# A MoE kernel's startup: where the last decoded weight tiles put their scratch, and when four of them are decoded

## The chip, the cores and the metric

One core of a Trainium2 chip runs the whole program. The metric is the device time of one execution in microseconds; before the change it is 847.33 us, the median of three runs (847.04 to 848.21).

## What is computed

The reference is a delta-rule attention, followed by two mixture layers on its output:

```
for t in range(S):                       # 4 batches x 8 heads, S = 768, D = 48
    y[t]  = q[t] @ state
    state = state + beta[t] * outer(k_n[t], v[t] - k_n[t] @ state)
x   = y as 3072 tokens x 384
h   = ((x @ w1) * (x @ w2)) @ w3         # 384 -> 1024 -> 1024
x2  = h @ w_out                          # 1024 -> 384
e   = argmax(x2 @ w_gate + bias[modality])          # 8 experts, one per token
out = gate[e] * (relu(x2 @ e_w1[e]) @ e_w2[e])
```

The weights w1, w2, w3 and w_out are stored as 8-byte floats, the rest as 4-byte floats.

## The kernel before

**The stages.** `startup` (L528) loads and decodes the 8-byte weights, multiplies w3 with w_out ahead of time (so that only one product, called w34, is left), computes the first attention step and prepares the inverse matrices of the first two pairs of steps. Then `moe1` (L720) runs for twelve blocks of 256 tokens: block i computes x @ w1, x @ w2, their product and the product with w34 for the tokens of step i, while `slot` (L165) issues the attention of step i + 1 between these matmuls. At the end `moe2` runs the experts. Each block of `moe1` has eight parts, f = 0 to 7, called eighths here. An eighth takes 128 of the 1024 hidden columns: 18 matmuls into one PSUM tile `pAB` (two halves, w1 and w2), then ScalarE's copy `a`, VectorE's product `a`, ScalarE's cast `ch`, VectorE's remainder `cl`. Its six matmuls with w34 (`px`) follow two eighths later (LAG = 2).

**The order of instructions.** All five engines issue in the order in which the Python code is written (the class `Engine`, L77 to L91, chains every instruction to the one before on its engine, so all rows of the profile stand at L84). The order around the change is set by the list `todo` of 36 tiles (L543 to L549) and by `tick(n)` (L653), which decodes one of them:

- `issue` (L557) starts DMAs from the SP queue. A tile lands in a buffer `raw` that is borrowed: the six places that later hold the second halves of w1 and w2 (`w010` to `w112`), and `x0`, `x1`, `xr`. A place of the first kind can be borrowed only by tiles up to the one that will be stored there (`last`, L551), so the last tiles of the list have few places, and each waits for the decode that gives one back.
- `scalar(n + 1)` (L582) has ScalarE write two things for the next tile: its magnitude `mag` and its low words, the latter into one of four slots of the SBUF tile `TT[1]`, called `sc` (slot n % 4).
- `vector(n)` (L598) combines them with two VectorE instructions.
- `use(n)` (L606) consumes the decoded tile: a w3 tile is read by four matmuls (`pw`), each of the w1 and w2 tiles is split into a high part by ScalarE and a low part by VectorE one tick later (`flush`, L647).

The tiles of w3 and w1/w2 alternate from tile 16 on. Numbers in this text: tile 28 and tile 30 are the last two of w3, the tiles 29 and 31 to 35 are the six of the second half of w1 and w2 (needed from eighth 4 of block 0 on).

**Where mag lives.** Ten tiles use the PSUM pool `pc`. The others use the tag `AB`, two PSUM banks, the same two that `pAB` of all blocks uses. Only the last tile, 35, has it in a slot of `sc`, two slots away from its own:

```
if n < FC + 2:
    mag[n] = self.pc.tile([P, DCH], F32, tag="pc", name="mag")
elif n <= NSTART:
    mag[n] = pm.tile([P, DCH], F32, tag="AB", name="mag", bufs=2)
else:
    mag[n] = sc[:, (n + 2) % 4]
```

**What block 0 still decodes.** `REST = (1, 1)`: tile 34 in eighth 0 and tile 35 in eighth 1 of block 0. VectorE also takes steps of the inverse of the second pair of attention steps there (`self.work`; two tensor_tensor rows `tmp` and `Tt` each); `PLAN1` says how many in each eighth, 21 in all.

**What the SP queue holds behind the tiles.** After the DMA of tile 35 come two tiles of keys (`kb`), the queries `W` of step 1 and step 2 (two DMAs each, one for each half of the partitions), and the values of step 2 (`vt`). The queries of step 1 are read by the matmuls `pq`, which stand on TensorE between eighth 1 and eighth 2 of block 0.

Of the kernel before, what the change touches and what calls it, by code (L numbers as in the profile page):

```python
# [51 lines left out]
PLAN = (0, 0, 3, 4, 5, 2, 1, 3), (2, 0, 4, 3, 4, 2, 0, 1)  # L52

MID = (0,) * 5 + (0, 0, 1) + (2, 2, 2, 1, 1, 1, 1, 2)
PLAN1 = (3, 4, 4, 3, 3, 2, 1, 1)
WORK1 = {0: 2, 1: 2, 2: 3, 3: 3, 4: 3, 5: 3}
AHEAD, W0 = 8, 0
CHAIN, GRAMS = (1, 1, 1, 1, 1, 1), (-6, -5, -3, -2)
START0 = (3, 3, 3, 3, 3, 3, 3)

REST = (1, 1)
EARLY = {2: 1, 3: 1, 4: 2, 5: 4, 6: 4, 7: 4}
LEAD = 1
LAG = 2
# [39 lines left out]
class Kernel:  # L104
# [423 lines left out]
    def startup(self):  # L528
# [14 lines left out]
        todo = [("o", g) for g in range(FC)] + w3s[:AHEAD] + w12[:W0]  # L543
        w12, n = w12[W0:], 0
        for x in range(AHEAD, K3):
            k = x + 1 - AHEAD
            todo += [w3s[x]] + w12[n:k]
            n = k
        todo += w12[n:]  # L549
        NSTART = len(todo) - sum(REST)  # L550
        last = {f"w{m}1{kk}": todo.index(("w", (m, 1, kk))) for kk in range(KC) for m in range(2)}  # L551
# [30 lines left out]
        def scalar(n):  # L582

            if n < len(todo):
                L, Hw, _ = raw[n]
                if n < FC + 2:
                    mag[n] = self.pc.tile([P, DCH], F32, tag="pc", name="mag")
                elif n <= NSTART:
                    mag[n] = pm.tile([P, DCH], F32, tag="AB", name="mag", bufs=2)
                else:  # L590
                    mag[n] = sc[:, (n + 2) % 4]
                mag[n] = mag[n][:, :L.shape[-1]]

                nc.scalar.activation(mag[n], Hw.bitcast(F32), AF.Abs, scale=2.0 ** -112)

                nc.scalar.activation(out[n].bitcast(I32), L.bitcast(U32), AF.Copy, scale=2.0 ** -29 * (1 - 2.0 ** -16), bias=7.5 * 2.0 ** -16 - 0.5)

        def vector(n):  # L598
            L, Hw, tag = raw.pop(n)
            o, stt = out[n].bitcast(I32), nc.vector.scalar_tensor_tensor  # L600
            stt(out=o, in0=mag[n].bitcast(I32), scalar=3, in1=o, op0=ALU.logical_shift_left, op1=ALU.bitwise_or)
            stt(out=o, in0=Hw, scalar=-2147483648, in1=o, op0=ALU.bitwise_and, op1=ALU.bitwise_or)
            if tag != "x0" or n < FC:
                free.append(tag)
# [42 lines left out]
        def flush(n):  # L647
            now = [f for due, f in after if due <= n]
            after[:] = [x for x in after if x[0] > n]
            for f in now:  # L650
                f()

        def tick(n):  # L653
            self.n = n
            if n >= NSTART:
                flush(n)
            scalar(n + 1)
            vector(n)
            flush(n)
            issue()  # L660
            use(n)

        def split(g):

            next(g)
            after.append((self.n + 1, lambda: list(g)))
# [9 lines left out]
        for g in grams:  # L676
            next(g)
        do = {-1: [lambda: scalar(0)], 0: [lambda: list(grams[0])], 1: [lambda: list(grams[1]), lambda: list(grams[2])], 2: [lambda: list(grams[3])],
              FC - 4: [lambda: self.queries(0), lambda: self.values(0), self.routing_loads],
              FC - 2: [lambda: self.keys(1)],  # L680
              FC + 3: [lambda: split(self.masked(0))], FC + 5: [lambda: self.tokens(0), lambda: self.values(1)]}
# [12 lines left out]
        for x in range(0, NU, HP):  # L694
            do.setdefault(FC + len(START0) + GRAMS[x // HP], []).append(lambda x=x: split(self.gram(1, x)))
        c = FC + len(START0)
        do.setdefault(c + 1, []).append(lambda: setattr(self, "work", self.inverse(1)))
        for n, k in WORK1.items():
            do.setdefault(c + 1 + n, []).extend([lambda: next(self.work)] * k)
        rs = self.routing_setup()  # L700
        for x in range(3):
            do.setdefault(FC + 8 + x, []).append(lambda: next(rs, None))
# [2 lines left out]
        for n in range(-1, NSTART):  # L705
            if n >= 0:
                tick(n)
            for f in do.get(n, ()):
                f()

        def rest():
            for n in range(NSTART, len(todo)):
                tick(n)
                yield
            flush(len(todo))

        flush(NSTART)
        self.rest = rest()

    def moe1(self, i):  # L720
# [3 lines left out]
        for f in range(FC):  # L724
# [16 lines left out]
            nc.scalar.copy(ch, a)  # L741
            steps = (PLAN1 if i == 0 else PLAN[(i + LEAD) % US])[f]
            if steps:
# [15 lines left out]
            if f == 6 and i + 1 < NT // MT:  # L759
                self.parts_x(i + 1)  # L760
            for _ in range(REST[f] if i == 0 and f < len(REST) else 0):
                next(self.rest, None)
            if i == 0 and f == len(REST):
                list(self.rest)
# [590 lines left out]
```

## Time and profile before

| | |
|---|---|
| median of three runs | 847.33 us |
| the profiled execution's own time | 850.87 us |
| its span, first to last instruction | 849.2 us |
| TensorE (PE) busy | 796.1 us, 94% of the span |
| VectorE (DVE) busy | 610.1 us, 72% |
| ScalarE (ACT) busy | 407.1 us, 48% |
| mean granted TensorE clock | 0.968 of full speed |

Times in all rows are counted from the first instruction. PE means TensorE's matmuls and PEld its weight loads; a row of the timeline gives the start, the length, the engine, the operation with output and inputs, the shape, how many equal instructions it merges, and, in brackets, how long the engine was idle before it and what ended that. A plain fp32 matmul of the program appears as two PE rows. DMA rows on the SP queue show the issue, not the transfer.

### The profile page before, as it was taken

To read this page: it belongs to the slowest core of one execution; us is meant where nothing else is said; L and a number is where in the kernel's file an instruction comes from. 1 tells how busy PE (TensorE), PEld (TensorE's weight loads), DVE (VectorE), ACT (ScalarE), POOL (GpSimd) and SP (SyncE) were. 2 spreads that over 40 slices of the span, in tenths; PEclk is the share of its full clock that TensorE was granted. 3 is DMA by queue.
4 is the path that set the end of the run, shared out by engine and by line. 5 is a ranking of instruction groups with operands and counts; after the bars stand their busy time and mean duration, and the time that the engine had idled before them with its cause. 6 is when DMAs were issued, how large, how long until landed. Compare 5 with 4: busy or idle time off the path is not lost.

```text
span 849.2 us, 24808 instructions
## 1 busy us (share of the span) xinstructions
PE 796.1 (94%) x10223; PEld 739.2 (87%) x10223; DVE 610.1 (72%) x1517; ACT 407.1 (48%) x859; POOL 160.8 (19%) x167
## 2 busy tenths in 40 slices
PE   5796789999999999999999999999899999999994
PEld 5564459999999999999999999999899999999983
DVE  5998899669856975697589854467785678677651
ACT  6357573561446244615452353334454655555541
POOL 5001201100001000000100000003244654645420
PEclk8599899999999999999999999999999999999998
DMA  9843463203120412132112301037457778666610
GB/s 299 288 152 97 125 182 108 74 22 103 66 67 29 126 40 64 37 117 62 41 41 62 102 2 40 21 117 238 143 168 223 241 229 266 222 219 229 236 59 7
DMA packets 48777, 105.42 MB, mean 124 GB/s; under 512 B 9412, under 2 KB 28756, under 8 KB 48656
## 3 DMA queue, kind: packets, MB, share of 16 engines
q1 hardware_dynamic: 41424, 88.35, 33.3%
q0 software_dynamic: 4064, 11.06, 3.8%
q10 hardware_dynamic: 3168, 4.34, 1.4%
q8 instruction: 82, 1.34, 0.7%
q14 instruction: 39, 0.32, 0.1%
HBM read 89.15 MB, written 10.63 MB: 118 GB/s over the span
## 4 chain that ended last, share of the span: by engine, by line
PE 67%; DVE 12%; issue 9%; POOL 4%; ACT 4%; DMA 3%; SPq 0%; POOLq 0%; ACTq 0%; DVEq 0%
PE pAB L84 23%; PE px L84 13%; PE ph L84 7%; PE spy L84 4%; PE py L84 3%; PE pu L84 3%; PE pq L84 2%; PE pk L84 2%; PE pg L84 2%; PE pw L84 2%; DVE TT L84 2%; PE pS L84 2%; POOL w1l L84 2%; PE pe L84 1%; POOL out_dram L84 1%
## 5 line engine op out<-in xcount | busy, mean ns | idle before, releaser
L84 PE MATMUL pAB<-x,w 128*128 128x256 f32 x1728 | 231.3, 288 | 2.7 <-DVE a L84 2.6
L84 PEld LDWEIGHTS pAB<-x,w 128*128 128x128 f32 x1728 | 214.4, 191 | 7.0 <-DVE a L84 2.8
L84 DVE TENSOR_TENSOR a<-a,pAB 128x256 f32<-128x256 f32 x96 | 40.0, 417 | 84.7 <-ACT a L84 84.4
L84 ACT COPY a<-pAB 128x256 f32<-128x256 f32 x96 | 35.7, 372 | 134.4 <-PE pAB L84 113.7
L84 ACT CAST ch<-a 128x256 fp32r<-128x256 f32 x96 | 38.9, 406 | 104.6 <-DVE a L84 104.6
L84 PE MATMUL ph<-sxh,w1h 128*128 128x256 f32 x288 | 82.7, 287 | 0.5 <-DVE hl L84 0.5
L84 ACT ACTIVATE hh<-ph 128x256 fp32r<-128x256 f32 x96 | 37.0, 385 | 94.2 <-PE ph L84 93.9
L84 PE MATMUL ph<-sxh,w1l 128*128 128x256 f32 x288 | 81.6, 283 | 0.0
L84 PE MATMUL ph<-sxl,w1h 128*128 128x256 f32 x288 | 81.6, 283 | 0.0
L84 DVE SCALAR_TENSOR_TENSOR hl<-ph,hh 128x256 fp32r<-128x256 f32 x96 | 40.3, 419 | 42.9 <-ACT hh L84 41.6
L84 DVE TENSOR_TENSOR tmp<-Ab,Tt 128x31 f32<-128x31 f32 (+15 forms) x186 | 67.1, 361 | 3.0
L84 DVE TENSOR_TENSOR Tt<-tmp,Tt 128x31 f32<-128x31 f32 (+15 forms) x186 | 63.9, 343 | 6.4
L84 DVE TENSOR_TENSOR w2l<-r,w2h 128x768 fp32r<-128x768 f32 x56 | 58.7, 1060 | 12.5 <-ACT w2h L84 12.2
L84 PE MATMUL px<-w34h,ch 128*128 128x392 f32 x192 | 65.6, 342 | 0.0
L84 PE MATMUL px<-w34h,cl 128*128 128x392 f32 x192 | 65.3, 340 | 0.0
L84 PE MATMUL px<-w34l,ch 128*128 128x392 f32 x192 | 65.2, 339 | 0.0
L84 POOL TENSOR_TENSOR w1l<-r,w1h 128x512 fp32r<-128x512 f32 x39 | 51.1, 1328 | 49.8 <-ACT w1h L84 49.6
L84 PEld LDWEIGHTS ph<-sxh,w1h 128*128 128x128 f32 x288 | 54.9, 191 | 1.3 <-DVE hl L84 1.1
L84 PEld LDWEIGHTS ph<-sxh,w1l 128*128 128x128 f32 x288 | 55.2, 192 | 0.0
L84 PEld LDWEIGHTS ph<-sxl,w1h 128*128 128x128 f32 x288 | 54.9, 191 | 0.0
L84 DVE TENSOR_TENSOR cl<-a,ch 128x256 fp32r<-128x256 f32 x96 | 40.4, 421 | 20.1 <-ACT ch L84 19.3
L84 ACT CAST w1h<-r 128x512 fp32r<-128x512 f32 x84 | 49.4, 616 | 2.3 <-DMA r<-in_e_w_dram 1.9
(263 smaller groups left out, 1678.4 us busy)
## 6 DMA issues: line engine op xcount, KB each, us to landing
r<-in_e_w_dram SPq DMA_DIRECT2D x42, 512.0 KB, 4.8
r<-in_e_w_dram SPq DMA_DIRECT2D x56, 384.0 KB, 3.9
raw<-in_w_dram SPq DMA_DIRECT2D x28, 512.0 KB, 3.9
kT<-in_kt_dram SPq DMA_DIRECT2D x12, 512.0 KB, 4.6
W<-in_q_dram SPq DMA_DIRECT2D x24, 256.0 KB, 4.2
vt<-in_v_dram SPq DMA_DIRECT2D x12, 384.0 KB, 4.2
kb<-in_kb_dram SPq DMA_DIRECT2D x12, 384.0 KB, 3.2
x2d<-xr ACTq DMA_DIRECT2D x22, 192.5 KB, 2.9
```

Source lines behind the costliest of these rows:

```text
L84: x = f(*a, **kw)
```

## The change

Tile 31 onward has its magnitude in `sc` instead of an `AB` bank. Four tiles instead of two are decoded in block 0: one in eighth 0, one in eighth 1, two in eighth 2. The list is reordered so that the last two tiles of w3 come as tiles 28 and 29, and the six tiles of the second half of w1 and w2 follow as tiles 30 to 35. From tile 30 on a tick first flushes what is due (the split of the tile before), then decodes. The steps of the inverse in block 0 are dealt out anew, 21 as before.

```diff
-PLAN1 = (3, 4, 4, 3, 3, 2, 1, 1)
+PLAN1 = (2, 2, 1, 4, 4, 4, 4, 0)
...
-REST = (1, 1)
+REST = (1, 1, 2)
+W0S = 1
...
         for x in range(AHEAD, K3):
-            k = x + 1 - AHEAD
+            k = min(x + 1 - AHEAD, 6)
             todo += [w3s[x]] + w12[n:k]
             n = k
...
-                elif n <= NSTART:
+                elif n < NSTART - 1:
                     mag[n] = pm.tile([P, DCH], F32, tag="AB", name="mag", bufs=2)
                 else:
                     mag[n] = sc[:, (n + 2) % 4]
...
         def tick(n):
             self.n = n
-            if n >= NSTART:
+            if n >= NSTART - 2:
                 flush(n)
             scalar(n + 1)
             vector(n)
...
-        do.setdefault(c + 1, []).append(lambda: setattr(self, "work", self.inverse(1)))
+        do.setdefault(c + W0S, []).append(lambda: setattr(self, "work", self.inverse(1)))
         for n, k in WORK1.items():
-            do.setdefault(c + 1 + n, []).extend([lambda: next(self.work)] * k)
+            do.setdefault(c + W0S + n, []).extend([lambda: next(self.work)] * k)
...
-        flush(NSTART)
         self.rest = rest()
```

NSTART is the number of tiles less the sum of REST: 34 before, 32 now. W0S = 1 leaves the start of the second inverse where it was. One line more at the top of the file makes L84 into L85.

The order of the rows on TensorE, on the SP queue and on GpSimd is the same as before, name by name; what differs there is which tile a `raw` or `pw` row belongs to. ScalarE and VectorE are reordered, and the prediction speaks of three places.

ScalarE, end of startup, from the magnitude of tile 32 to the first copy `a` of block 0 (`mag` is a PSUM bank, `TT_95` is `sc`, a CAST to `w_...` is the high part of a w1 or w2 tile), before:

```order
L84 ACTIVATE mag<-raw 128x512
L84 ACTIVATE TT_95<-raw 128x512
L84 ACTIVATE mag<-raw 128x512
L84 ACTIVATE TT_95<-raw 128x512
L84 CAST w_1184<-TT_95 128x512
L84 ACTIVATE mag<-raw 128x512
L84 ACTIVATE TT_95<-raw 128x512
L84 CAST w_1192<-TT_95 128x512
L84 CAST w34h<-pw 128x392
L84 CAST w_1200<-TT_95 128x512
L84 COPY a<-pAB 128x256
```

The same place in the change, from the magnitude of tile 30:

```order
L85 ACTIVATE mag<-raw 128x512
L85 ACTIVATE TT_95<-raw 128x512
L85 CAST w34h<-pw 128x392
L85 ACTIVATE TT_95<-raw 128x512 x2
L85 CAST w_1173<-TT_95 128x512
L85 ACTIVATE TT_95<-raw 128x512 x2
L85 COPY a<-pAB 128x256
```

The two rows "x2" are magnitude and low words of tile 31 and of tile 32, both now in `sc`. Tile 33 and tile 34 are no longer ahead of block 0.

VectorE, from the remainder `R` of attention step 1 through eighth 0 of block 0 and the start of eighth 1, before:

```order
L84 TENSOR_TENSOR R<-vt,pk 128x384 x2
L84 TENSOR_TENSOR a<-a,pAB 128x256
L84 TENSOR_TENSOR tmp<-Ab,Tt 128x252
L84 TENSOR_TENSOR Tt<-tmp,Tt 128x14x18
L84 TENSOR_TENSOR cl<-a,ch 128x256
L84 SCALAR_TENSOR_TENSOR TT_95<-mag,TT_95 128x512
L84 SCALAR_TENSOR_TENSOR TT_95<-raw,TT_95 128x512
L84 TENSOR_TENSOR tmp<-Ab,Tt 128x255
L84 TENSOR_TENSOR Tt<-tmp,Tt 128x15x17
L84 TENSOR_TENSOR tmp<-Ab,Tt 128x256
L84 TENSOR_TENSOR Tt<-tmp,Tt 128x16x16
L84 TENSOR_TENSOR a<-a,pAB 128x256
```

The change, with the three rows ahead of `R` (low part of tile 30, decode of tile 31):

```order
L85 TENSOR_TENSOR w_1173<-TT_95,w_1173 128x512
L85 SCALAR_TENSOR_TENSOR TT_95<-TT_95 128x512
L85 SCALAR_TENSOR_TENSOR TT_95<-raw,TT_95 128x512
L85 TENSOR_TENSOR R<-vt,pk 128x384 x2
L85 TENSOR_TENSOR a<-a,pAB 128x256
L85 TENSOR_TENSOR tmp<-Ab,Tt 128x252
L85 TENSOR_TENSOR Tt<-tmp,Tt 128x14x18
L85 TENSOR_TENSOR cl<-a,ch 128x256
L85 TENSOR_TENSOR w_1182<-TT_95,w_1182 128x512
L85 SCALAR_TENSOR_TENSOR TT_95<-TT_95 128x512
L85 SCALAR_TENSOR_TENSOR TT_95<-raw,TT_95 128x512
```

Ahead of `R` VectorE has the tiles up to 31 now, 33 before; the decodes of tiles 32 and 33, three low parts and the remainder of the last w34 slice stand in the eighths 0 to 2.

VectorE, from eighth 2 of block 0 to the last low part, in the change (before, the last low part stood in eighth 2, ahead of the `a` of eighth 3):

```order
L85 TENSOR_TENSOR cl<-a,ch 128x256
L85 TENSOR_TENSOR w_1304<-TT_95,w_1304 128x512
L85 SCALAR_TENSOR_TENSOR TT_95<-TT_95 128x512
L85 SCALAR_TENSOR_TENSOR TT_95<-raw,TT_95 128x512
L85 TENSOR_TENSOR w_1425<-TT_95,w_1425 128x512
L85 SCALAR_TENSOR_TENSOR TT_95<-TT_95 128x512
L85 SCALAR_TENSOR_TENSOR TT_95<-raw,TT_95 128x512
L85 TENSOR_TENSOR a<-a,pAB 128x256
L85 TENSOR_TENSOR tmp<-Ab,Tt 128x247
L85 TENSOR_TENSOR Tt<-tmp,Tt 128x19x13
L85 TENSOR_TENSOR cl<-a,ch 128x256
L85 TENSOR_TENSOR w_1430<-TT_95,w_1430 128x512
```

Tiles 34 and 35 are decoded in one eighth, and the last low part (`w_1430`, tile 35) stands behind the `cl` of eighth 3.

## Rows read from the trace of the kernel before

**Rows 1.** Busy time by stretch: PE, PEld, DVE, ACT, POOL, then PEclk, DMA share, GB/s
```profile
135.00:160.00 25.00, 25.00 (x388) 23.66 (x385) 22.27 (x49) 9.40 (x23) 3.40 (x3) 1.00 0.37 113
```

**Rows 2.** Timeline of TensorE, end of startup and block 0 up to eighth 4
```profile
108.08 3.46 PE L84 MATMUL pw<-wosW,TT 128*128 128x392 f32 x10
...
114.42 2.90 PE L84 MATMUL pw<-wosW,TT 128*128 128x392 f32 x8 [0.91 <-DVE TT L84]
...
120.50 2.07 PE L84 MATMUL pk<-X,kT 64*64 64x48 f32 x64
122.70 2.39 PE L84 MATMUL pAB<-x,w 128*128 128x256 f32 x18
127.71 3.59 PE L84 MATMUL pAB<-x,w 128*128 128x256 f32 x18 [2.62 <-DVE a L84]
131.23 2.19 PE L84 MATMUL pu<-R,TT 64*64 64x48 f32 x58
133.20 0.27 PE L84 MATMUL pq<-W,kT 64*64 64x64 f32 x2
...
135.21 2.41 PE L84 MATMUL pAB<-x,w 128*128 128x256 f32 x18
137.47 0.34 PE L84 MATMUL px<-w34h,ch 128*128 128x392 f32 x1
...
143.87 2.41 PE L84 MATMUL pAB<-x,w 128*128 128x256 f32 x18
```

**Rows 3.** Timeline of VectorE, same stretch
```profile
119.33 0.69 DVE L84 SCALAR_TENSOR_TENSOR TT<-raw,TT 128x512 int32<-128x512 int32 x1
...
124.63 0.69 DVE L84 TENSOR_TENSOR w<-TT,w 128x512 fp32r<-128x512 f32 x1 [1.35 <-ACT w L84]
...
126.31 1.01 DVE L84 TENSOR_TENSOR R<-vt,pk 128x384 f32<-128x384 f32 x2
127.24 0.41 DVE L84 TENSOR_TENSOR a<-a,pAB 128x256 f32<-128x256 f32 x1
127.57 0.41 DVE L84 TENSOR_TENSOR tmp<-Ab,Tt 128x252 f32<-128x252 f32 x1
...
137.83 2.85 DVE L84 TENSOR_TENSOR W<-pq,mask 64x512 f32<-64x512 f32 x4
...
142.00 0.69 DVE L84 TENSOR_TENSOR w<-TT,w 128x512 fp32r<-128x512 f32 x1
```

**Rows 4.** Timeline of ScalarE, same stretch
```profile
122.83 0.67 ACT L84 ACTIVATE mag<-raw 128x512 f32<-128x512 f32 x1 [1.75 <-DMA raw<-in_w_dram]
123.40 0.68 ACT L84 ACTIVATE TT<-raw 128x512 int32<-128x512 uint32 x1
...
128.00 1.26 ACT L84 ACTIVATE TT<-raw 128x512 f32<-128x512 f32 x2
...
132.50 0.61 ACT L84 CAST w<-TT 128x512 fp32r<-128x512 f32 x1
```

**Rows 5.** Timeline of the SP queue: issues of tiles 34, 35, the second half of W
```profile
117.69 0.33 SPq L84 DMA_DIRECT2D raw<-in_w_dram  x1
...
120.11 0.33 SPq L84 DMA_DIRECT2D raw<-in_w_dram  x1
...
122.65 0.59 SPq L84 DMA_DIRECT2D W<-in_q_dram  x1
```

**Rows 6.** Tile raw, issue to landing, 100 to 135 us
```profile
DMA to landing us min/median/max: 3.9/4.3/5.1
```

**Rows 7.** Tile W, issue to landing, of the issue at 122.65 alone
```profile
DMA to landing us min/median/max: 7.3/7.3/7.3
```

**Rows 8.** Busy time by stretch, columns as in rows 1: two stretches at half clock
```profile
80.80:87.40 6.60, 5.04 (x8) 2.52 (x8) 6.25 (x19) 1.25 (x2) 0.00 (x0) 0.50 0.29 81
...
128.60:131.80 3.20, 3.20 (x24) 2.98 (x24) 3.06 (x8) 1.03 (x3) 0.00 (x0) 0.50 0.94 208
```

**Rows 9.** Timeline of TensorE, the idle time ahead of the first of them
```profile
82.36 1.68 PE L84 MATMUL pw<-wosW,TT 128*128 128x392 f32 x2 [4.87 <-DVE TT L84]
```

## The prediction

> **What bounds the kernel now.** I read busy time by stretch first. From 135 us on TensorE is busy all 25.00 of 25.00 us [rows 1]: what shifts the start of that stretch shifts the end by as much, if later waits stay as they are. So the change is judged by when eighth 2 of block 0 starts, 135.21 [rows 2], and by any new hole behind it. TensorE's timeline shows the holes ahead of it: the decode-bound w3 products (0.91 us idle before 114.42), and, between eighth 0 (122.70) and eighth 1 (127.71), 2.62 us that ended with VectorE's `a` [rows 2]: eighth 1 takes the same PSUM bank as eighth 0, since the magnitude of tile 34 still holds the other one. VectorE's and ScalarE's timelines show why that `a` is late. ScalarE waited 1.75 us for tile 34 to land, so VectorE waited 1.35 us for ScalarE's cast, and R and `a` stand behind that [rows 3, 4]. After the hole the granted clock is 0.50 for 3.2 us [rows 8], and eighth 1 takes 3.59 instead of 2.41 us [rows 2]: 1.2 us more.
>
> **What goes.** The bank wait goes, since no magnitude from tile 31 on is in PSUM, and so does the wait for tile 34 ahead of block 0. VectorE has less to do ahead of R: two decodes (0.69 + 0.72 each), three low parts (0.69 each, issued 0.6 apart) and a w34 remainder, some 5 us, stand in eighths 0 to 2. That alone would start R 5 us earlier. It does not, because of what comes in its place.
>
> **What is late next, first: tile 31 waits for TensorE.** Slot (31 + 2) % 4 = 1 holds tile 29, which is now the last w3 tile. ScalarE may overwrite it with tile 31's magnitude only when TensorE's four matmuls have read tile 29. The two tiles 28 and 29 are now one run on TensorE. Such a run took from 108.08 to 113.51 (0.91 before 114.42), 5.43 us [rows 2]. VectorE's decode of tile 29 comes two tiles (2 x 2.0 us) ahead of tile 31's end at 120.02, at about 116, and the second half of the run needs it at 114.42 + 2.7 = 117.1: no wait. So the run ends at 114.42 + 5.43 = 119.85. Behind it:
> - TensorE: `pk` takes 2.20 (120.50 to 122.70), so eighth 0 starts at 122.0, 0.7 earlier. Eighth 1 follows after 2.26 (135.21 to 137.47), at 124.3, 3.4 earlier and at full clock; `pu` follows, until 128.5 (2.0 us, 131.23 to 133.20) [rows 2].
> - ScalarE idles until 119.85, then magnitude and low words (1.26) and the cast (0.61) [rows 4]: 121.7. VectorE: low part (0.69), then the decode of tile 31 (0.72 + 0.69) [rows 3], until 123.75. The steps overlap by 0.1 each, so 123.6 to 123.8. Before, this decode ended at 119.33 + 0.69 = 120.02 [rows 3].
>
> **What is late next, second: the queries.** The decode of tile 31 gives back the place into which tile 35 lands: before, its DMA was issued at 120.11, right behind 120.02 [rows 3, 5]. SP's order is unchanged, so keys, queries W and values stand behind that DMA. Now it goes out at 123.7 to 123.9, 3.7 us later. Before, the second half of W was issued at 122.65 and landed 7.3 us later, at 129.95, unnoticed, since `pq` started at 133.20 [rows 2, 5, 7]. From tile 35's issue that is 9.84. Now `pq` is reached at 128.5 and W lands at 123.8 + 9.84 = 133.6, if the DMAs take as long. They may take less, since tile 34's transfer (issued 117.69) no longer overlaps tile 35's: a tile alone takes 3.9, the median here is 4.3 and the longest 5.1 [rows 6]. At most the spread between longest and least, 1.2, with 1.0 more if issues behind tile 35 no longer wait for `pk`, comes off: 131.4. I take 132.8, nearer the measured sum. Then the second half of `pq` and eighth 2 follow: 132.8 + 2.0 = 134.8 against 135.21: **-0.4** (bounds -1.8 and +0.4).
>
> **Third: the clock.** TensorE then idles from 128.5 to 132.8, but for one matmul pair: 4.3 us. After 4.87 us of idle, ahead of 82.36, the clock was 0.50 until 87.4, 5 us of work [rows 8, 9]; after 2.62 us it was 0.50 for 3.2 us [rows 2, 8]. At half clock eighth 1 lost 1.18 us in about 2.7, 0.44 per us. Half clock for `pq` alone costs between nothing (`pu` began inside the second stretch and took its 2.0 us) and 2.0 x 0.44 = 0.9 [rows 2, 8], say 0.4; for 5 us from 132.8 it costs that and 0.44 x 2.5 to 3 = 1.1 to 1.3 on eighths 2 and 3. Bounds 0 (a stretch that ends before `pq` does) and 2.0; 4.3 is nearer to 4.87 than to 2.62, so I stay near the upper sum: **+1.3**. The Trainium skill ("TensorE: Matmul & The Clock Gate", "Part 1: The HAM clock gate") has half rate as the state to which TensorE falls back when idle, and has activity release it again; the rows here agree in direction (1.00 before, 0.50 after both holes). It speaks against a change that makes one hole of 4.3 us out of one of 2.6.
>
> **Fourth: the last low part.** Its two matmuls stand at the end of eighth 4. Before, it was written at 142.00 to 142.69, and eighth 4 started at 143.87 [rows 2, 3]: cover of over 1 us. Now, counted from eighth 2's start F: `a` at F + 2.9 (18 matmuls, ScalarE's copy), then VectorE's two `a`, two `cl`, two inverse steps (two rows of 0.41 each), two decodes (1.4 each) and three low parts (0.69), 8.2 us, less 0.6 of overlap, plus 0.7 in which VectorE waits for ScalarE's low words and cast (1.26 + 0.61 against the decode's 1.4) [rows 3, 4]: F + 11.2. The matmul that reads it is due at F + 8.66 (135.21 to 143.87) + 2.1 = F + 10.8. **+0.4** (0 to 0.8).
>
> **At nothing.** Magnitude in SBUF: ScalarE's pair of rows took 1.26 with both in SBUF (128.00) against 0.67 + 0.68 less the overlap with the magnitude in PSUM (122.83, 123.40), 1.25 [rows 4]. The Trainium skill ("ScalarE: Activation LUTs", "What happens when an exp ACTIVATE runs") says that ScalarE writes PSUM faster than SBUF. By the rows that is 0.01 per tile, 0.04 for the four tiles moved. The steps of the inverse moved to eighths 3 to 6 lie beside full TensorE; if VectorE ran late there, `a` of the next eighth would show it. The w34 remainder moved to eighth 1 is read by the first `px` in eighth 2, behind the wait for W.
>
> **Sum.** -0.4 + 1.3 + 0.4 = +1.3 us. Against the profiled execution's 850.87 that is 852.2. The median of the runs is 847.33, 3.5 below the profiled one; I carry the difference over: **848.6 us**.
>
> **The rivals.** What a measurement of this kernel can tell from no change is about 0.2%, 1.7 us.
> - *The long hole (0.34, slower).* W lands at 133.6 or TensorE's clock stays at 0.50 until eighth 3. Place: `pq`, then eighths 2 and 3. Price: +0.4 instead of -0.4, clock +2.0, last low part +0.4: +2.8 us, 850.1. It decides once the wait before `pq` exceeds 4.9 us, the idle time after which 5 us of work ran at half clock [rows 8, 9]. For it: the full 9.84 is what was measured. Against it: in that stretch the SP queue was also loaded by tile 34. It is the clock page's rule carried through.
> - *Early queries (0.06, faster at best by little).* If W lands by 131.0, no long hole opens. Then VectorE sets the pace: from R at 123.8 to the last low part it has R (1.0), four `a` and four `cl` (0.41 each), six inverse steps (0.83), five low parts, four decodes, the w34 remainder (0.5) and the masks of `pq` (2.85) [rows 3], 21.7 us, less 1.6 of overlap (0.08 in each of some 20 rows that need not wait for the one before, as at 127.57), plus the 0.7: 144.6. Eighth 4 would then end near 144.9, against 143.87 + 2.26 = 146.1 before: -1.2 us, 846.1. A gain over 1.7 us needs more than this floor leaves.
> - *The bank is not the wait (within the forecast's case).* If eighth 1 still shared a bank with eighth 0, it would start after `a`, some 0.7 us later; `pq` waits for W all the same, so no time changes.
>
> **Chances.** Forecast, within 0.2%: 0.60. The long hole, slower: 0.34. Early queries or less: 0.06, of which I give faster by over 0.2% 0.05 and put the rest to no change. The range holds both sides: 846.1 at VectorE's floor, and 850.1 for the long hole, with 0.5 for a W later still: 846.1 to 850.6. The forecast's own range is 847.0 to 849.0.
>
> **What would show it.** In the profile after: ScalarE idle about 4 us ahead of tile 31's magnitude, released by TensorE's `pw`; SP's issue of tile 35 near 123.8; eighth 1 right behind eighth 0 with no wait for `a`; TensorE idle ahead of `pq`, released by the DMA of W, 3 to 5 us; a stretch at 0.50 after it; some 0.4 us idle in eighth 4 before its last matmuls; from there on the same work as before. Wrong would be: `pq` without a wait (then W lands sooner than any row says), eighth 2 before 133 or after 137, or a difference that arises after block 0.

## The result and the profile after

The change takes 854.15 us, median of four executions (853.62 to 854.69), against 847.77 for the kernel before beside it (847.04 to 848.68): ratio 1.0066, 95% interval 1.0053 to 1.008. It is slower, and outside the range of the prediction (846.1 to 850.6). A second set of six executions gave 853.28, ratio 1.0055 (1.0035 to 1.0075).

| | before | after |
|---|---|---|
| the profiled execution's own time | 850.87 us | 854.55 us |
| its span | 849.16 us | 852.75 us |
| start of eighth 0, eighth 2, eighth 5 | 122.70, 135.21, 149.28 | 122.42, 137.73, 152.98 |
| eighth 5 to the start of block 1 | 15.81 | 15.80 |
| block 1 | 44.39 | 47.38 |
| blocks 2 to 10 | 355.68 | 355.68 |
| experts, first to last product | 236.47 | 233.28 |

The time was lost in two places, block 0 and block 1. The profiled pair differs by only 3.7 us, since the experts' stage, whose instructions are the same, was 3.2 us shorter in the execution of the change. What differs there is TensorE's clock. Before, it fell to 0.50 behind a wait for VectorE that ended at 604.69, and again at 640; after, it fell once, at 607, and that time ahead of the same wait, which took the loss up (0.27 us idle there instead of 1.85). In the profiles of all fifteen further runs, experiments included, the stage took 233.1 to 236.7, the least with no such fall (run 13) or with one that a wait took up (run 2), the most with two (run 4). How many an execution gets differs between profiles of one kernel (two before, one in run 1), so I don't count the 3.2 to the change; whether the change shifts the odds is not shown.

**Block 0.** The timeline of TensorE after the change, to be read against [rows 2]. In this execution everything comes 0.5 us later before the change has any part in it (the products at 108.08 there start at 108.61 here, those at 114.42 at 114.95), so 0.5 is to be taken off.

```profile
114.95 3.56 PE L85 MATMUL pw<-wosW,TT 128*128 128x392 f32 x10 [0.91 <-DVE TT L85]
...
120.42 2.07 PE L85 MATMUL pk<-X,kT 64*64 64x48 f32 x64
122.42 4.58 PE L85 MATMUL pAB<-x,w 128*128 128x256 f32 x36
126.92 2.07 PE L85 MATMUL pu<-R,TT 64*64 64x48 f32 x64
133.03 0.47 PE L85 MATMUL pq<-W,kT 64*64 64x64 f32 x2 [4.04 <-DMA W<-in_q_dram]
134.13 3.67 PE L85 MATMUL pq<-W,kT 64*64 64x64 f32 x62 [0.63 <-DMA W<-in_q_dram]
137.73 3.12 PE L85 MATMUL pAB<-x,w 128*128 128x256 f32 x18
...
147.09 2.29 PE L85 MATMUL pAB<-x,w 128*128 128x256 f32 x17
149.58 0.39 PE L85 MATMUL pAB<-x,w 128*128 128x256 f32 x1 [0.20 <-DVE w L85]
...
```

Eighths 0 and 1 are one row of 36 matmuls now: the wait of 2.62 us between them is gone, as the change means it. In its place TensorE waits 4.04 and 0.63 us for W. What comes behind runs slowly: the 62 matmuls `pq` take 3.67 us, `pu`, of the same tile, 2.07 for 64. The stretch is at the lower of the clock's two levels, 1.2 GHz, as the busy time by stretch shows (columns as in [rows 1]; the second row is in block 1):

```profile
132.50:139.33 6.83, 5.67 (x71) 5.36 (x72) 4.40 (x8) 2.74 (x6) 0.00 (x0) 0.50 0.71 135
...
193.94:197.35 3.41, 3.41 (x57) 3.29 (x54) 3.09 (x14) 1.48 (x3) 0.00 (x0) 0.50 0.07 17
```

Why W is late, on ScalarE and on VectorE, to be read against [rows 3, 4]:

```profile
115.66 0.49 ACT L85 CAST w34h<-pw 128x392 fp32r<-128x392 f32 x1
120.52 1.23 ACT L85 ACTIVATE TT<-raw 128x512 f32<-128x512 f32 x2 [4.37 <-PE pw L85]
121.66 0.60 ACT L85 CAST w<-TT 128x512 fp32r<-128x512 f32 x1
123.02 1.26 ACT L85 ACTIVATE TT<-raw 128x512 f32<-128x512 f32 x2 [0.76 <-DVE w L85]
...
122.30 0.69 DVE L85 TENSOR_TENSOR w<-TT,w 128x512 fp32r<-128x512 f32 x1 [3.67 <-ACT w L85]
...
123.62 0.69 DVE L85 SCALAR_TENSOR_TENSOR TT<-raw,TT 128x512 int32<-128x512 int32 x1
124.23 1.01 DVE L85 TENSOR_TENSOR R<-vt,pk 128x384 f32<-128x384 f32 x2
```

Tile 31's magnitude waits for TensorE to have read tile 29, so its decode ends at 124.31 (123.62 + 0.69). On the SP queue the DMA of tile 35 goes out right behind that, and the second half of W behind it, against [rows 5]:

```profile
124.41 0.33 SPq L85 DMA_DIRECT2D raw<-in_w_dram  x1
...
126.27 0.59 SPq L85 DMA_DIRECT2D W<-in_q_dram  x1
```

W is there at 134.13: 9.7 us after tile 35's issue and 7.9 after its own, against 9.84 and 7.3 before [rows 5, 7].

**Block 1.** There TensorE waits 2.54 us ahead of the matmuls `pr` (0.90 in the kernel before, same place) and, in this execution, falls to 0.50 behind it:

```profile
193.20 0.18 PE L85 MATMUL pr<-oh,tri 128*128 128x8 bf16 x1 [2.54 <-DVE W L85]
```

Counted from the start of block 1, `pr` starts 1.8 us later than before; the half clock behind it adds 1.2. In runs 3 and 4, whose clock stays up there, block 1 takes 46.18.

`pr` waits for VectorE's masks on W. VectorE is late because of what stood on ScalarE 25 us earlier, at the end of block 0. The rows of ScalarE there, and of VectorE:

```profile
162.20 0.83 ACT L85 CAST x<-x 128x768 fp32r<-128x768 f32 x1
167.78 2.10 ACT L85 COPY TT<-TT 32x1024 f32<-32x1024 f32 x2 [4.76 <-DVE TT L85]
169.91 2.81 ACT L85 ACTIVATE An<-pg 128x512 f32<-128x512 f32 x6
172.75 0.37 ACT L85 COPY a<-pAB 128x256 f32<-128x256 f32 x1
...
163.93 2.03 DVE L85 STREAM_TRANSPOSE An<-Tt 128x1024 f32<-128x1024 f32 x1
165.80 1.95 DVE L85 STREAM_TRANSPOSE TT<-Tt 128x1024 f32<-128x1024 f32 x1
173.15 0.42 DVE L85 TENSOR_TENSOR a<-a,pAB 128x256 f32<-128x256 f32 x1 [5.40 <-ACT a L85]
```

and the same place on ScalarE in the kernel before (the first run below, where block 1 starts 4.4 us earlier):

```profile
160.09 2.79 ACT L84 ACTIVATE An<-pg 128x512 f32<-128x512 f32 x6
162.91 0.37 ACT L84 COPY a<-pAB 128x256 f32<-128x256 f32 x1
163.77 0.41 ACT L84 CAST ch<-a 128x256 fp32r<-128x256 f32 x1 [0.48 <-DVE a L84]
164.08 2.10 ACT L84 COPY TT<-TT 32x1024 f32<-32x1024 f32 x2
```

The last of the 21 steps of the second inverse is a copy of `TT` on ScalarE. PLAN1 put it into eighth 7, behind that eighth's gram copies `An<-pg` and its `a`; the change's PLAN1 ends 4, 0 and puts it into eighth 6, ahead of both. Its two transposes on VectorE come late too, because four steps stand in each of the eighths 3 to 6. So ScalarE idles 4.76 us with 2.81 us of gram copies ready behind it, VectorE idles 5.40, and R, the router and the masks of block 1 follow late.

### The profile page after: what moved, and what is told of

It reads as the page before. It is cut to its first block, busy times and chain, and to the rows that moved or that the text cites. A ratio compares the mean times of both kernels' runs of the same rounds, so it can differ in the third digit from the quotient of the medians.

```text
span 852.8 us, 24803 instructions
## 1 busy us (share of the span) xinstructions
PE 798.0 (94%) x10223; PEld 741.0 (87%) x10223; DVE 609.6 (71%) x1517; ACT 407.6 (48%) x859; POOL 160.8 (19%) x167
## 4 chain that ended last, share of the span: by engine, by line
PE 69%; DVE 13%; issue 6%; DMA 5%; ACT 4%; POOL 1%; SPq 1%; ACTq 0%; DVEq 0%; POOLq 0%
PE pAB L85 21%; PE px L85 14%; PE ph L85 9%; PE spy L85 5%; PE pw L85 3%; PE pq L85 3%; PE py L85 3%; DVE TT L85 2%; PE pk L85 2%; PE pu L85 2%; PE pg L85 2%; PE pS L85 2%; DMA W<-in_q_dram 2%; DVE tmp L85 1%; DMA r<-in_e_w_dram 1%
## 5 line engine op out<-in xcount | busy, mean ns | idle before, releaser
L85 PE MATMUL pAB<-x,w 128*128 128x256 f32 x1728 | 231.1, 288 | 0.2 <-DVE w L85 0.2
L85 PEld LDWEIGHTS pAB<-x,w 128*128 128x128 f32 x1728 | 214.3, 191 | 4.6 <-DVE w L85 0.4
L85 DVE TENSOR_TENSOR a<-a,pAB 128x256 f32<-128x256 f32 x96 | 40.0, 417 | 87.9 <-ACT a L85 87.6
L85 ACT COPY a<-pAB 128x256 f32<-128x256 f32 x96 | 35.7, 371 | 133.5 <-PE pAB L85 119.4
L85 ACT CAST ch<-a 128x256 fp32r<-128x256 f32 x96 | 38.9, 406 | 101.5 <-DVE a L85 101.5
L85 PE MATMUL ph<-sxh,w1h 128*128 128x256 f32 x288 | 82.4, 286 | 0.5 <-DVE hl L85 0.5
L85 PE MATMUL ph<-sxh,w1l 128*128 128x256 f32 x288 | 81.1, 282 | 0.0
L85 PE MATMUL ph<-sxl,w1h 128*128 128x256 f32 x288 | 81.0, 281 | 0.0
L85 ACT ACTIVATE hh<-ph 128x256 fp32r<-128x256 f32 x96 | 37.0, 385 | 89.2 <-PE ph L85 84.2
L85 DVE TENSOR_TENSOR tmp<-Ab,Tt 128x31 f32<-128x31 f32 (+15 forms) x186 | 66.9, 360 | 2.9
L85 DVE TENSOR_TENSOR w2l<-r,w2h 128x768 fp32r<-128x768 f32 x56 | 59.7, 1078 | 12.2 <-ACT w2h L85 9.9
L85 DVE TENSOR_TENSOR Tt<-tmp,Tt 128x31 f32<-128x31 f32 (+15 forms) x186 | 63.8, 343 | 6.4
L85 DVE SCALAR_TENSOR_TENSOR hl<-ph,hh 128x256 fp32r<-128x256 f32 x96 | 40.2, 419 | 39.1 <-ACT hh L85 34.5
L85 PE MATMUL px<-w34h,ch 128*128 128x392 f32 x192 | 65.6, 342 | 0.0
L85 PE MATMUL px<-w34h,cl 128*128 128x392 f32 x192 | 65.3, 340 | 0.0
L85 PE MATMUL px<-w34l,ch 128*128 128x392 f32 x192 | 65.2, 339 | 0.0
L85 POOL TENSOR_TENSOR w1l<-r,w1h 128x512 fp32r<-128x512 f32 x39 | 50.8, 1321 | 50.0 <-ACT w1h L85 49.4
L85 PEld LDWEIGHTS ph<-sxh,w1h 128*128 128x128 f32 x288 | 54.7, 190 | 1.3 <-DVE hl L85 1.1
L85 DVE TENSOR_TENSOR cl<-a,ch 128x256 fp32r<-128x256 f32 x96 | 40.4, 421 | 20.1 <-ACT ch L85 18.4
L85 PEld LDWEIGHTS ph<-sxh,w1l 128*128 128x128 f32 x288 | 54.6, 190 | 0.0
L85 PEld LDWEIGHTS ph<-sxl,w1h 128*128 128x128 f32 x288 | 54.5, 189 | 0.0
L85 ACT CAST w1h<-r 128x512 fp32r<-128x512 f32 x84 | 49.5, 615 | 3.7 <-DMA r<-in_e_w_dram 3.2
```

Source lines behind the costliest of these rows:

```text
L85: x = f(*a, **kw)
```

## The experiments

Lengths in the table come from TensorE's timeline of each profiled execution: eighth 0 of block 0 to block 1, and block 1. The first column names the runs as below; times are medians, ratios are to the kernel before, beside it on the same chip. Eighth 0 starts anywhere from 121.59 to 124.16, because the startup ahead of it differs between executions (the products at 108.08 [rows 2] start at 107.30 to 109.87). In the kernel before, the later startup has the shorter block 0 (run 1), so lengths of block 0 compare well only between runs that start up alike.

| run | time | ratio (95%) | block 0 | block 1 |
|---|---|---|---|---|
| 1: before, again | 848.18 | 0.9995 (0.9986 to 1.0005) | 40.24 | 44.39 |
| change | 854.15 | 1.0066 (1.0053 to 1.008) | 46.36 | 47.38 |
| 13: change, again | 853.28 | 1.0055 (1.0035 to 1.0075) | 46.04 | 47.51 |
| 2: queries first | 851.07 | 1.0033 (1.0022 to 1.0045) | 43.54 | 46.92 |
| 3: tile 31 in PSUM | 851.57 | 1.0027 (1.0006 to 1.0047) | 42.03 | 46.18 |
| 4: hole filled | 854.21 | 1.0063 (1.0044 to 1.0082) | 44.11 | 46.18 |
| 14: hole filled, again | 853.01 | 1.0053 (1.0034 to 1.0072) | 43.65 | 47.36 |
| 5: end of PLAN1 undone | 852.32 | 1.0058 (1.0042 to 1.0074) | 45.57 | 44.39 |
| 15: both of these | 851.24 | 1.0028 (1.0014 to 1.0043) | 44.15 | 44.39 |
| 8: runs 2, 3 and 5 in one | 849.70 | 1.0023 (1.001 to 1.0036) | 43.46 | 44.39 |
| 12: and lighter early steps | 847.52 | 0.9984 (0.9972 to 0.9995) | 40.82 | 44.39 |
| 6: before, end of PLAN1 alone | 848.71 | 1.0016 (1.0004 to 1.0027) | 42.26 | 44.40 |
| 7: before, bank alone | 847.89 | 1.0001 (0.9991 to 1.0011) | 40.25 | 44.39 |
| 9: bank alone, mended | 847.32 | 0.9988 (0.9972 to 1.0004) | 39.75 | 44.39 |
| 10: and queries first | 847.23 | 0.9988 (0.9976 to 1.0001) | 40.01 | 44.39 |
| 11: and masks first | 844.08 | 0.9947 (0.9928 to 0.9967) | 38.07 | 44.39 |

**1. The kernel before once more.**

> The kernel before, unchanged. The change made the medians 6.4 us longer, but the two profiled executions only 3.7 (850.87 to 854.55), since the profiled execution of before lay 3.1 above its median. Theory A, the profiled execution of before drew something that most executions don't have (a stretch at half clock in block 0, or a wait further on): another profile comes at 847 to 848.5, and its timeline shows that place shorter by some 3 us. Theory B, profiling itself adds 3 us to this kernel: the new profile is again near 850.9 with the same holes.

The median stays, but its profile shows what one profile can't: the hole between the eighths 0 and 1 was 1.94 us here, no half clock followed it, and block 0 took 40.24 us instead of 42.39. The profile on which the prediction rests was an execution with a long block 0, but with an early one too: here eighth 0 starts at 124.16, 1.46 us later, and block 1 at 164.40, only 0.7 us earlier. Of the 2.4 us between the two spans the larger part, 1.7, lies in the experts' stage (236.47 there, 234.75 here).

**2. Queries ahead of tile 35.**

```diff
-                self.queries(1)
                 self.queries(2)
...
+        do.setdefault(NSTART - 2, []).append(lambda: self.queries(1))
```

> The change, with the two DMAs of the queries of step 1 issued ahead of tile 35's instead of behind it and behind both key tiles. Theory A, the wait for W and the half clock after it are the loss: W lands by 125, pq follows pu without a wait, no stretch at 0.50 in block 0, eighth 2 starts at about 131 instead of 137.7; then VectorE sets the pace with some 2 to 3 us of holes in eighth 4; in all 4 to 5 us less than the change, so within 0.2% of before. Theory B, the loss is VectorE's, which has the same work to do in block 0: then the hole moves to eighth 4 in full and the time stays at that of the change, 854.

The matmuls `pq` follow `pu` without a wait and at full clock, and eighth 2 starts at 129.80 instead of 137.73. Only part of that lasts, since eighth 4 now waits for its own weights:

```profile
129.80 2.42 PE L85 MATMUL pAB<-x,w 128*128 128x256 f32 x18
...
140.35 0.50 PE L85 MATMUL pAB<-x,w 128*128 128x256 f32 x2 [0.91 <-ACT w L85]
...
143.69 0.50 PE L85 MATMUL pAB<-x,w 128*128 128x256 f32 x2 [1.52 <-ACT w L85]
```

Block 0 is 2.8 us shorter than the change's and the time 3.1 us less, where 4 to 5 was expected. By the medians no other single mend gives more, so the late queries are the largest loss of the change; block 1 keeps its own.

**3. Tile 31's magnitude in PSUM.**

```diff
-                elif n < NSTART - 1:
+                elif n < NSTART:
```

> The change, with tile 31's magnitude back in a PSUM bank; tiles 32 to 35 stay in SBUF. Theory A, tile 31's wait for TensorE's reading of tile 29 is the first cause: ScalarE's 4.4 us of idle ahead of tile 31 go, tile 35's DMA goes out some 2.7 us earlier (at about 121 to 121.5), W lands about 130.5, TensorE idles 2 us ahead of pq instead of 4.7, and the time falls by 3.5 to 5 us against the change. Theory B, the position of W behind three other transfers is enough for the loss: W lands as late as before and the time falls by less than 1 us.

Tile 35's DMA goes out at 122.72, in an execution whose startup is 1.3 us later than the change's; there it was 124.41. The waits for W shrink to 0.48 and 0.77 us, and eighth 2 starts at 133.86. Eighth 4 waits 1.23 us for ScalarE's split, block 1 takes 46.18. So the wait for TensorE is what made W late. The time is 2.6 us less than the change's, where 3.5 to 5 was expected; the ten executions spread from 848.6 to 853.3.

**4 and 14. The hole filled with matmuls that nobody reads.**

```diff
             if s == 1:
+                for _ in range(26):
+                    self.nc.tensor.matmul(self.xt[0][:, 0:XW], self.w34[0][:, 0, 0:P], self.w34[0][:, 0], start=True, stop=True)
                 list(self.masked(s))
```

> The change, with 26 matmuls of 128x392 put between pu and pq, whose result nothing reads: TensorE works through the wait for W. They take 26 x 0.178 = 4.6 us, about the wait. Theory A, half clock after the hole is a loss of its own: no stretch at 0.50, pq takes 2.0 instead of 3.7 and eighth 2 2.4 instead of 3.1, the time falls by about 2.4 us against the change. Theory B, the clock falls for another reason, or what it costs is taken up by the later wait for VectorE in eighth 4: the time stays within 0.7 us of the change.

> The change once more, unaltered, as the measure for the two runs beside it. Every theory: 854.2, ratio 1.0066 within its interval (1.0053 to 1.008). A median under 853 would say that the first four executions were a slow draw and that part of the loss to explain is none.

> The fourth run once more: 26 matmuls whose result nobody reads fill TensorE's hole ahead of pq; nothing else of the change is altered. Theory (the hole of 4 us costs its half clock on top of its wait): the profile shows pq in 2.0 us instead of 3.7 and eighth 2 some 2.3 us earlier, and the time is 1.5 to 3 us under the change's beside it. Rival (the half clock is not what sets the time: what is gained in block 0 is waited for again at pr, since VectorE is no earlier): within 0.8 us of the change's, as the first six executions had it (854.2).

In both profiles the clock stays at 1.00 through block 0 and `pq` takes 2.1 us; in the second, block 0 is 2.4 us shorter than in the change beside it. The time does not follow: 854.21 against the change's 854.15, and 853.01 against 853.28 beside it, with executions from 849.81 to 856.15. In these profiles `pr` waits 2.68 us and the experts' stage takes 236.7 and 235.6 us instead of 233.3. The first of the two has two falls of the clock in that stage. The executions that were not profiled show only their mean granted clock, and the spread goes with it: in the second set the four longest (854.59 to 856.15) have 0.964 to 0.966, six of the other seven 0.968 to 0.972. In which stage they lost it is open.

**5 and 15. The end of PLAN1 undone, alone and with the hole filled.**

```diff
-PLAN1 = (2, 2, 1, 4, 4, 4, 4, 0)
+PLAN1 = (2, 2, 1, 4, 4, 4, 3, 1)
```

> The change with one step of the second inverse moved back: PLAN1 ends 4, 3, 1 instead of 4, 4, 0, so that ScalarE's two copies of TT stand behind the gram copies An and behind the a and ch of eighth 7 again, as in the kernel before. Block 0 up to eighth 6 is left as the change has it, with its wait for W. Theory (the step's place holds ScalarE and VectorE up by some 3 us at the end of block 0, and TensorE pays at pr in block 1): block 1 takes 44.4 us again (change 47.4, 46.2 to 46.9 in its variants), the wait ahead of pr is 0.9 instead of 2.2 to 2.7, and the time is 854.2 - 1.8 to 3.0 = 851.2 to 852.4. Rival (VectorE is late in block 1 because of block 0's late weights, whatever the order of the steps): block 1 stays at 46 to 47.4 and the time at 854.

> The end of PLAN1 mended (as in the fifth run) and the hole filled (as in the fourth) together. With the wait at pr gone (0.9 us, block 1 at 44.4), what the hole's half clock costs must show in the time: theory 852.3 - 1.5 to 2.5 = 849.8 to 850.8. Rival (the half clock costs nothing that lasts): 852.3, as the fifth run.

Block 1 takes 44.39 us again, and the wait at `pr` is that of the kernel before, in both:

```profile
190.26 0.18 PE L85 MATMUL pr<-oh,tri 128*128 128x8 bf16 x1 [0.89 <-DVE W L85]
```

One step's place was worth 3 us of block 1 in the profiles. In the time less is shown: by the medians run 5 is 1.0 to 1.8 us under the change's two, but its ratio, 1.0058, lies between theirs (1.0055 and 1.0066). With the hole filled as well the time falls to 851.24, 2.0 under the change beside it, all eleven executions (849.21 to 851.75) below all six of the change (852.50 to 854.05). Between run 5 and run 15 only the filled hole differs: 1.1 us by the medians, where 1.5 to 2.5 was expected, and 1.4 us in the length of block 0. The two were not timed side by side.

**6. The end of PLAN1 alone, in the kernel before.**

```diff
-PLAN1 = (3, 4, 4, 3, 3, 2, 1, 1)
+PLAN1 = (3, 4, 4, 3, 3, 2, 2, 0)
```

> The kernel before with nothing changed but the end of PLAN1 (2, 0 instead of 1, 1): the two copies of TT come ahead of the gram copies of eighth 7. No tile, bank or DMA is touched. Theory: block 0 as before up to eighth 6, pr in block 1 waits 2.2 to 2.7 us instead of 0.9, block 1 takes 46.2 or more instead of 44.4, and the time is 848.2 + 1.8 = 850.0, or up to 851.2 if the longer hole brings a stretch at half clock. Rival: no change, 848.2, block 1 at 44.4.

The theory in its plain form falls: block 1 takes 44.40 us. ScalarE has the copy ahead of the gram copies here too, but it waits little:

```profile
160.45 2.10 ACT L84 COPY TT<-TT 32x1024 f32<-32x1024 f32 x2 [0.77 <-DVE TT L84]
162.58 2.81 ACT L84 ACTIVATE An<-pg 128x512 f32<-128x512 f32 x6
```

The first transpose ran at 153.96 already, since most steps were done in the eighths 0 to 4. So the order costs only together with late transposes. In the change they are late behind the 4, 4, 4, 4 of its PLAN1; what the four decodes add to that was not tried apart. The ratio, 1.0016, is below what this comparison can place; nothing in blocks 0 and 1 answers to it.

**7 and 9. The bank alone, in the kernel before.**

```diff
-                elif n <= NSTART:
+                elif n < NSTART:
...
-            if n >= NSTART:
+            if n >= NSTART - 1:
```

Run 7 has the first pair of lines only; tile 32's split reads what tile 34's magnitude left there. Run 9 has both.

> The kernel before with nothing changed but the place of tile 34's magnitude (SBUF instead of the second bank of pAB): the order of tiles, the DMAs and the steps of the inverse are those of before. Theory (the bank is what eighth 1 waits for): eighth 1 follows eighth 0 without the wait for a of 1.9 to 2.6 us; pq is reached about 2 us earlier and now meets W, which landed near 130, so that 0 to 0.8 us of the gain is lost there; eighth 2 starts 1.2 to 2.6 us earlier and the time is 848.2 - 1.2 to 2.6 = 845.6 to 847.0. Rival (VectorE's decode of tile 33 and R hold up the same stretch, the bank only shows it): the hole moves to pu or pq, eighth 2 starts as before, time 848.2.

> The seventh run's edit (tile 34's magnitude in SBUF in the kernel before) with the split of tile 32 flushed ahead of tile 34's magnitude, so that all weights are right (in the seventh run tile 34's magnitude came over tile 32 before its split, so that one weight tile held wrong numbers). Theory from the seventh run's trace: the hole ahead of eighth 1 goes (1.9 to 2.6 us), but pq then waits some 0.7 us for W, and py of eighth 3 for VectorE's masks on W, which stand behind four steps of the inverse: eighth 4 starts as before, time 847.8 within 0.5. Rival: the wrong order of the seventh run hid a gain, time 846 or less.

Eighth 1 follows eighth 0 at once, and the gain is given back, where run 7 was expected at 845.6 to 847.0: in run 9 by the wait for W alone,

```profile
130.66 2.08 PE L84 MATMUL pq<-W,kT 64*64 64x64 f32 x62 [0.76 <-DMA W<-in_q_dram]
132.67 2.42 PE L84 MATMUL pAB<-x,w 128*128 128x256 f32 x18
```

and in run 7 also at `py`, which waits for VectorE's masks, so that eighth 3 takes 6.03 us instead of 5.34. Block 0 is 0 to 0.5 us shorter than in the first run, the ratios are 1.0001 and 0.9988. By the medians what the change set out to remove was worth 0 to 1 us by itself; the interval of run 9 (0.9972 to 1.0004) reaches to 2.4. Run 9 starts eighth 0 at 122.80, as the profiled kernel before does (122.70), and beside that one its block 0 is 2.6 us shorter: there the hole was longer and had a half clock behind it.

**10 and 11. Bank, queries, then masks.** Run 10 is run 9 with `queries(1)` issued as in run 2; run 11 also has

```diff
-PLAN1 = (3, 4, 4, 3, 3, 2, 1, 1)
+PLAN1 = (1, 3, 3, 5, 4, 3, 1, 1)
```

> The ninth run's kernel with the queries of step 1 issued ahead of tile 35 too. Theory: the wait of pq for W goes and eighth 2 starts another 0.7 us or more earlier, but the masks end no sooner, since they stand behind the same rows of VectorE: py waits by as much longer, eighth 4 starts as in the ninth run, time 847.8 within 0.7. Rival: W was the bound, time 847.1 or less with py not waiting.

> The tenth run's kernel with four steps of the inverse moved behind the masks (PLAN1 = 1, 3, 3, 5, 4, 3, 1, 1 instead of 3, 4, 4, 3, 3, 2, 1, 1; its end is unchanged). Theory: with bank, queries and VectorE's rows ahead of the masks all out of the way, eighths 0 to 4 run without a hole, eighth 4 starts 1.3 to 2.3 us earlier than in the kernel before, block 1 is not touched (44.4), time 845.5 to 846.5, ratio 0.997 to 0.9985. Rival: the last low part (tile 35) becomes the wait in eighth 4, gain under 0.7, time 847.1 or more.

Runs 7, 10 and 11 start up alike (109.32 to 109.52). Run 10: eighth 2 starts 1.5 us earlier than in run 7, without a wait, but eighth 4 only 0.3; `py` waits in turn, 0.72, 0.32 and 0.29 us, for masks that VectorE starts at 138.75:

```profile
139.59 0.30 PE L84 MATMUL py<-W,X 128*64 128x64 f32 x2 [0.72 <-DVE W L84]
140.22 1.15 PE L84 MATMUL py<-W,X 128*64 128x64 f32 x32 [0.32 <-DVE W L84]
```

Run 11: the masks start at 136.09, no wait is left, and busy time by stretch from eighth 0 to block 1 has TensorE busy all of 38.07 us at full clock:

```profile
123.78:161.85 38.07, 38.07 (x632) 36.29 (x628) 34.86 (x74) 17.90 (x40) 4.72 (x5) 1.00 0.48 136
```

Its median, 844.08, is below the expected 845.5 to 846.5, 4.3 us under the kernel before and 10.1 under the change. Block 0 is 2.2 us shorter than in the first run, whose eighth 0 starts alike; why the median gains 4.3 is not accounted for (the profiled execution, 845.30, is one of its longer ones). It is the fastest kernel of this study. Three waits stood in a row; each one that was removed uncovered the next, and little was gained before the third went. Neither the early queries nor the new PLAN1 was tried alone in the kernel before, so what each is worth without the others is not shown.

**8 and 12. The change with its three losses mended, and lighter early steps.** Run 8 has the edits of 2, 3 and 5; run 12 also has PLAN1 = 1, 1, 1, 4, 5, 5, 3, 1.

> The change with three things mended at once: queries of step 1 issued ahead of tile 35 (as in the second run), tile 31's magnitude in PSUM (as in the third), PLAN1 ending 4, 3, 1 (as in the fifth). If the three losses are separate, block 0 runs as in the second run or better (block 1 starts at 165.1 or up to 2.4 us, the two holes of its eighth 4, earlier), block 1 takes 44.4 instead of 46.9, and the time is 851.1 - 2.5 = 848.6 down to 846.2: level with the kernel before, or better by the part of eighth 4's holes that goes. If something of the change that none of the three names costs time too, it stays above 849.

> The eighth run's kernel (the change with queries first, tile 31 in PSUM and the end of PLAN1 mended) with two steps of the inverse fewer ahead of the last decodes (PLAN1 = 1, 1, 1, 4, 5, 5, 3, 1 instead of 2, 2, 1, 4, 4, 4, 3, 1). It asks what makes eighth 4 wait 0.92 and 1.52 us for its weights there. Theory A (VectorE has too many rows ahead of the four decodes): two steps are 4 rows of some 0.45 us, 1.8 us; the two holes shrink by 1 to 1.8 us and the time is 847.9 to 848.7. Theory B (magnitudes in SBUF make ScalarE wait for VectorE's low part of the tile two before, 0.76 to 0.89 us per tile, and VectorE for ScalarE's cast, so that the four decodes take their time whatever stands between): the holes stay within 0.5 us of 2.4, time 849.2 to 850.2.

The losses are not quite separate. Run 8 is 849.70, above the 849 that was named as the sign of a fourth loss: eighth 4 keeps both of its waits for weights, 0.92 and 1.52 us, with a fall of the clock behind them. ScalarE's rows show why:

```profile
126.82 1.27 ACT L85 ACTIVATE TT<-raw 128x512 f32<-128x512 f32 x2 [0.79 <-DVE w L85]
...
131.48 1.25 ACT L85 ACTIVATE TT<-raw 128x512 f32<-128x512 f32 x2 [0.89 <-DVE w L85]
...
138.53 1.24 ACT L85 ACTIVATE TT<-raw 128x512 f32<-128x512 f32 x2 [0.80 <-DVE w L85]
```

With its magnitude in `sc` a tile waits for VectorE's low part of the tile two before (the same slot), and that low part waits for ScalarE's cast. Four tiles decoded in this way, between the rows of the eighths, end behind the first matmuls of eighth 4. In run 12 the first of the two waits is gone, as theory A has it (0.19 us are left, for a low part); the second is 1.52 as before, as theory B has it. No half clock follows it here. Run 12's startup was 2.1 us later than run 8's, and how much of the shorter wait is due to that can't be told from two profiles. The time, 847.52, is below what either theory had; the ratio falls from 1.0023 to 0.9984. The change so mended is 1 us better than the kernel before beside it, and stays behind run 11 (0.9947), which decodes two tiles in block 0 and not four; that this makes the difference was not tried by itself.

## Why the prediction was wrong

Counted with the 0.5 us taken off, eighth 5 starts 3.2 us later than before; the prediction's sum is +1.3. Block 1 adds 3.0 us, which it did not have. 847.8 + 3.2 + 3.0 = 854.0, against a median of 854.15. That it meets the median so closely is in part luck: against run 1, where the startup came 1.4 us later (109.50 for 108.08) and eighth 5 still started 0.7 us earlier (148.59), the 3.2 would be 5.3. Two steps of the prediction failed, the half clock on `pq`, put at 0.4, and the moved steps of the inverse, put at nothing; the landing of W was 0.8 us off besides.

- **Right: what goes, and what is late next.** The bank wait went; ScalarE waited 4.37 us for `pw`; the decode of tile 31 ended at 123.8 (124.31 less 0.5), inside 123.6 to 123.8; tile 35's DMA was issued at 123.9; TensorE waited for W ahead of `pq`, and a half-clock stretch came behind it. Run 3 shows the first link, run 2 the second.
- **W at 132.8: 0.8 us too early.** It was there at 133.6 (134.13 less 0.5), 9.72 behind tile 35's issue, against the measured sum of 9.84: next to nothing came off. I took off 0.8 for a queue that tile 34 no longer loads. The issues behind tile 35 did go out faster (1.9 us to W's second half, 2.5 before [rows 5]), but W's own DMA took 7.9 us, and 7.3 before [rows 7].
- **`pq` at half clock: 1.6 us, not 0.4, and over my bound of 0.9.** This is the term that failed in block 0. I read from `pu` at 131.23, which took its 2.0 us, that small matmuls lose little at half clock; but that stretch ended at 131.8 [rows 2, 8], so `pu` had run mostly at full clock. 62 matmuls of 64x64 take 3.67 us at 1.2 GHz here and 2.08 at 2.4 GHz in run 9, 1.76 times as long; `pg` goes the same way in run 2 (3.22 for 64 that lie for the most part in the slow stretch after eighth 4, 2.08 in the change). The Trainium skill ("TensorE: Matmul & The Clock Gate", "Part 1: The HAM clock gate") gives 107 ns against 56 for a bf16 matmul of 128 columns, cold and warm, 1.9 times; the rows, 1.76 for a smaller fp32 matmul, agree nearly, and by that rule the 2.0 us would have been estimated at 3.8.
- **Eighths 2 and 3: +0.7** (3.12 against 2.41), where 0.9 was left for them. **Last low part:** eighth 4 took 5.89 us against 5.41, +0.5 for the predicted +0.4.
- **"At nothing" for the moved steps of the inverse: 3.0 us.** The text says that they lie beside full TensorE and names the `a` of the next eighth as what would show otherwise. That `a` is the row at 172.75 above. What I had not followed is the last step's instruction on ScalarE: which rows stand behind it there, and when its input is ready. Run 5 shows that it is this step, run 6 that the late transposes belong to it. The prediction counted VectorE's rows of each step and left out ScalarE's. Of the 3.0, 1.8 is the late start of `pr` and 1.2 the half clock behind it.
- **The magnitude in SBUF**, also put at nothing, did cost nothing on ScalarE itself: a pair of rows took 1.23 and 1.26 us (at 120.52 and 123.02), against 1.25 before [rows 4].
- **The long hole**, at 850.1, had the place, and its price, 2.8 us, was near the 3.2 that block 0 cost: its terms were +0.4, +2.0 and +0.4, and +0.4, +2.3 and +0.5 came. Its condition, a wait of over 4.9 us, was not met (4.04 and 0.63); W at its full sum was. **Early queries** fell: W was late by all the measured sum.
- **The range.** It was built from waits in block 0 alone. The text named eighth 2 after 137 and a difference that arises after block 0 as what would prove it wrong. Both came: eighth 2 at 137.2, with the 0.5 off, and block 1.

## What to carry to other kernels

When a step is moved, follow every engine that it issues on, not the one on which it is long: ask for each what stands behind it in that engine's order and when its input is ready; here copies that waited 4.76 us for their input held up 2.8 us of ready work, and the bill came 25 us later on another engine. A freed buffer is worth only what lies between it and the next wait: by the medians the bank alone gave 0 to 1 us, the queries on top of it 0.1, and with the masks as well it was 4.3. And where a transfer is queued behind one that waits for a buffer, issue first what is due first.

## What the runs showed of the hardware that was not expected

A VectorE row of the inverse that takes 0.4 us took 1.3 and 1.7 us where it met a tensor_tensor of 768 elements on GpSimd, as in these rows of the change (VectorE's, then GpSimd's):

```profile
151.91 0.41 DVE L85 TENSOR_TENSOR a<-a,pAB 128x256 f32<-128x256 f32 x1
152.24 1.32 DVE L85 TENSOR_TENSOR tmp<-Ab,Tt 128x207 f32<-128x207 f32 x1
153.59 0.38 DVE L85 TENSOR_TENSOR Tt<-tmp,Tt 128x207 f32<-128x207 f32 x1
...
151.68 1.65 POOL L85 TENSOR_TENSOR vt<-vt,rb 128x768 f32<-128x768 f32 x1
```

The VectorE row ends within 0.3 us of GpSimd's, here and in run 12 (1.73 us beside 1.48). The row ahead of it, `a`, lies beside the same GpSimd instruction and took its usual 0.41 us; one of its inputs, `pAB`, is in PSUM. What the two engines share was not tried. The Trainium skill ("GPSIMD Engine Reference", "1. Specifications") has GpSimd's SBUF interface shared with VectorE, with contention where a VectorE instruction has two SBUF inputs; both slow rows have two, and the trace agrees.

After the same hole of 1.9 to 2.6 us ahead of eighth 1 the clock fell in two profiles of the old order of tiles (2.62 in the kernel before, 2.47 in run 6) and stayed at 1.00 in one (1.94, the first run). Whether its length or its moment decided is not settled; a hole's clock cost can't be read from one profile.
